# The last supertiles' units: second half rounded in two pieces, its subtraction and the fills put behind an addition

## The chip, the cores and the metric

The kernel runs on one core of a Trainium2 chip. TensorE (PE) multiplies matrices into PSUM; its weight loads have a row of their own in the profile (PEld). VectorE (DVE) and ScalarE (ACT) work element by element and read PSUM, GpSimd (POOL) does a little arithmetic and issues some DMAs, and SyncE (SP) issues the rest. Every engine executes its own instructions in order and waits for the others at semaphores. The metric is the time of one execution in microseconds; lower is better.

## The reference

An attention without softmax is followed by two feed-forward networks, each over all 2 x 3008 = 6016 tokens of width 256, with 2048 hidden columns:

```python
scores = scale * np.matmul(z, z.transpose(0, 2, 1))
attn = np.maximum(scores, 0.0) ** 2
out = np.matmul(attn, v)
x = u * out
...
h = x @ w_in1
g = h - np.tanh(h)
x = g @ w_out1
...
h = x @ w_in2
g = np.where(h >= 1, h, np.where(h <= -1, 0.0, (h + 1) ** 2 / 4))
return g @ w_out2
```

The weights come as 64-bit floats and are turned into 32-bit ones on the chip.

## The kernel before

After the attention (440 us of the span) the two networks run one after the other. The tokens are cut into six **supertiles** of 1024, the last of 896, and each supertile into two halves of columns: 512, and in the last supertile 448 (`w`). The 2048 hidden columns are cut into eight blocks of 256 (`f`). A **unit** is one block of one supertile of one network. Units are numbered through: the first network has units 0 to 47, its last supertile 40 to 47; the second has 48 to 94, its last supertile 88 to 94 (the very last block has code of its own, `end_s` and `end_av`).

A value is held as two parts, hi (rounded) and lo (the rest, by a subtraction), and a product takes three matmuls (`mult`). The four products of a 2 x 2 block multiplication are saved down to seven, by sums of blocks: Y holds A11, then has S2, S3 and A22 added to it one after another, X holds A12, and V holds S1 and later S4. Since Y goes on being added to, ScalarE takes a **snapshot** of it before each addition: m1 after A11, u2 after S2, u3 after S3 (`snap`; tiles `m` and `u` in the trace), and the half B takes a copy after A22 (`hb<-m`). VectorE adds: `ha<-m` is X + m1, `ha<-u` is V + u3, `hb<-u` is V + u2. TensorE may write S2 into Y only when m1 is taken, S3 only after u2, A22 only after u3, and S4 into V only after `ha<-u`.

The unit's two halves A and B (tiles `ha`, `hb`) then pass through the network's function in `Half`: `first` (tanh on ScalarE in the first network, a clamp on VectorE in the second), `square` (second network, ScalarE), `value` (VectorE, `ta` or `tb`), `round` (ScalarE, hi: `gha`, `ghb`), `rest` (VectorE, lo: `gla`, `glb`). Their products with `w_out` (`parts`) are multiplied in the next unit, between the next unit's own blocks: eight matmuls with gha after S2, four with gla and six with ghb after S3, two more with ghb and four with glb after S4. The six with ghb take its second 512 or 448 columns first (four matmuls), then the first (two).

The order is written out by hand in `emit`, with `self` the unit and `p` the one before it, whose half B is finished here. In the first network ScalarE rounds half A at the end of its own unit (`if not self.late`), ahead of the next unit's m1; in the second network it does so in the next unit, behind m1. Work that belongs to no unit is called by `fill`, twice in a unit: steps that prepare the next supertile's inputs (tiles `xh`, `xl`, `t`), the conversion of the second network's weights (`win`, `wout`, `ein`, `eout`, `min`, `mout`, `phin`, `plin`, `phout`, `plout`), and the transposes of finished output tiles (`ot<-y`). One unit in each supertile of the second network but its first, unit 89 in the last one, has `before` set and an order of its own, since two banks of the finished supertile are emptied in it.

Of the kernel before, what the change touches and what calls it, by code (L numbers as in the profile page):

```python
# [8 lines left out]
F32R = mybir.dt.float32r  # L9
# [6 lines left out]
P = 128  # L16
# [6 lines left out]
QT = 512  # L23
# [8 lines left out]
def attention_then_two_ffn(  # L32
# [40 lines left out]
    sp_p = ctx.enter_context(tc.tile_pool(name="split", bufs=3))  # L73
# [31 lines left out]
    def flush():  # L105
        for fn in deferred:
            fn()
        deferred.clear()
# [614 lines left out]
    def fill():  # L723

        if fills:
            step = fills.pop(0)
            for fn in step:
                if fn is not None:
                    fn()
            if len(step) == 1:  # L730
                work(CONVERT[1] / 2)
        else:
            work(CONVERT[1])
        due()

    def copy(out_, in_):
        nc.scalar.activation(out=out_, in_=in_, func=AF.Copy)  # L737

    def add(out_, x, bank):
        nc.vector.tensor_tensor(out=out_, in0=x, in1=bank, op=ALU.add)  # L740

    class Half:
# [26 lines left out]
                out=t, in0=self.h[self.at(j)], in1=t, op=ALU.subtract if self.net == 0 else ALU.max,  # L769
            )  # L770

        def round(self, js=(None,)):
            self.hi = sp_p.tile([P, 2, 512], F32R, tag="hi", name=f"gh{self.nm}")
            for j in js:
                copy(self.hi[self.at(j)], self.t[self.at(j)])

# [15 lines left out]
    class Unit:  # L792
# [59 lines left out]
        def emit(self, p, att=None):  # L852

            w = self.w
            before = p and p.net == 1 and p.f == 0 and p.s and p.before
            self.before = p
            self.late = self.net == 1 or att is not None
            one, two, three = p.parts_list if p else ([], [], [])
            Y = self.bank()
            self.mult(Y, A11, "b11", True)  # L860
            m1 = self.snap("m1", Y)
            if p and p.late:
                p.A.round()
            if p and p.before and p.before.net == 0:
                p.before.empty(0)
            X = self.bank()
            self.mult(X, A12, "b21", True)
            if p:
                if p.net == 1:
                    p.B.first()  # L870
                p.A.rest()
                p.B.first() if p.net == 0 else p.B.square(1 if before else None)
            if att:
                for fn in att[2][:5]:
                    fn()
            self.A = Half(self.net, w, "a")
            if not (p and p.late):
                add(self.A.h[:, 0, :w], m1, X[:, :w])
            V = self.bank()
            self.mult(V, S1, "t1", True)  # L880
            if att:
                for fn in att[2][5:]:
                    fn()
                got = []
                inside.append(lambda: self.mult(Y, S2, "t2"))
                inside.append(lambda: got.append(self.snap("u2", Y)))
                att[0]()
                u2 = got[0]
            else:
                self.mult(Y, S2, "t2")  # L890
                u2 = self.snap("u2", Y)
            if before:
                before.empty(1, lambda: p.B.square(0))
            if p:
                for j in (1, 0) if before else (None,):
                    p.B.value(j)
                if p.late:
                    add(self.A.h[:, 0, :w], m1, X[:, :w])
            for fn in one[:4] if before else one:
                fn()  # L900
            if p:
                p.B.round((1, 0) if before else (None,))
                if self.i > 1:
                    fill()
                else:
                    scales.pop()()
                    due()
                    due()
                p.B.rest()
            self.mult(Y, S3, "t3")  # L910
            if before:
                for fn in one[4:6] + two[:2] + one[6:]:
                    fn()
                two = two[2:]
            u3 = self.snap("u3", Y)
            add(self.A.h[:, 1, :w], u3, V[:, :w])
            if self.net == 1 or att:
                self.A.first()
            for fn in two:
                fn()  # L920
            if att:
                self.A.value()
                att[1]()
            if self.i > 1:
                fill()
            if self.net == 1:
                self.A.square()
            self.mult(Y, A22, "t4")
            self.mult(V, S4, "b22")
            self.B = Half(self.net, w, "b")  # L930
            if self.net == 0 and not att:
                self.A.first()
            copy(self.B.h[:, 1, :w], Y[:, :w])
            if not att:
                self.A.value()
            if att:
                flush()
            add(self.B.h[:, 0, :w], u2, V[:, :w])
            for fn in three:
                fn()  # L940
            if not self.late:
                self.A.round()
            if p and p.net == 1:
                p.empty(0)
            self.parts_list = self.parts()
# [178 lines left out]
    with tc.manual_schedule():  # L1124
# [64 lines left out]
        def work(amount):  # L1189

            if not (converts or posts):
                return
            state["credit"] = min(state["credit"] + amount, 2.0)
            if posts:
                cost, fn = posts.pop(0)
                fn()
                state["credit"] -= cost
            while converts and state["credit"] > 0 and len(posts) < 3:
                if state["step"] == 0:
                    next(converts[0])  # L1200
                elif state["step"] == 1 and len(converts) > 1:
                    next(converts[1])
                state["step"] += 1
                cost = next(converts[0], None)
                if cost is None:
                    converts.pop(0)
                    state["step"] = 1
                else:
                    state["credit"] -= cost
# [45 lines left out]
        def due():  # L1255

            now = [fn for k, fn in later if k <= 0]
            later[:] = [(k - 1, fn) for k, fn in later if k > 0]
            for fn in now:
                fn()  # L1260
# [73 lines left out]
        p = None  # L1334
        for i, (net, s, f) in enumerate(units):
            if f == 0:
                more = (net, s + 1) if (net, s + 1, 0) in units else (1, 0) if net == 0 else None
# [9 lines left out]
            p = u  # L1347
# [70 lines left out]
```

## Time and profile before

| | |
|---|---|
| time, median of 3 runs | 1420.18 us (1419.55 to 1420.5) |
| the profiled execution's own time | 1417.62 us |
| its span, first to last instruction | 1415.8 us |
| TensorE matmuls, weight loads busy | 99%, 83% |
| VectorE, ScalarE, GpSimd busy | 88%, 70%, 8% |
| granted TensorE clock, mean | 0.999 |

Matmuls are pipelined and their ends are modelled, so a matmul row of 0.37 us may stand beside the next one 0.20 us later. "Idle before" in a row is the time the engine stood still ahead of it, with what ended that time.

### The profile page before, as it was taken

How to read it: one execution, taken by the hardware profiler on the slowest of the kernel's cores; microseconds unless marked ns; L12 is line 12 of the kernel's file. 1: busy time of each engine (PE TensorE's matmuls, PEld its weight loads, DVE VectorE, ACT ScalarE, POOL GpSimd, SP SyncE). 2: the span in 40 equal slices, each digit the busy share in tenths (PEclk: the TensorE clock that was granted, in tenths of full speed). 3: DMA queues.
4: the chain of work that ended last, by engine and by line, in shares of the span. 5: the costliest groups of instructions: out<-in, count | busy, mean ns of one | idle time of the engine just before them, and what ended most of it. 6: DMA issues, size and time to landing. Idle time of an engine off the chain costs nothing.

```text
span 1415.8 us, 21846 instructions
## 1 busy us (share of the span) xinstructions
PE 1408.6 (99%) x8206; PEld 1173.7 (83%) x8206; DVE 1243.9 (88%) x1557; ACT 996.3 (70%) x1258; POOL 116.0 (8%) x169
## 2 busy tenths in 40 slices
PE   9999999999999999999999999999999999999998
PEld 7888888888888888888888889988888888888897
DVE  8888899788898989899889889989898898988887
ACT  8888758888765767667676767666666666666664
POOL 0111110022110010110201110000000000000000
PEclk9999999999999999999999999999999999999999
DMA  8788897599989557484847667572564653546461
GB/s 231 249 279 256 234 237 190 177 283 270 257 220 318 198 195 254 167 309 134 314 147 271 230 224 276 173 289 89 176 225 178 208 189 109 184 157 222 148 208 27
DMA packets 229546, 301.02 MB, mean 213 GB/s; under 512 B 111152, under 2 KB 166192, under 8 KB 229440
## 3 DMA queue, kind: packets, MB, share of 16 engines
q1 hardware_dynamic: 213088, 258.01, 57.6%
q0 software_dynamic: 11520, 40.96, 8.1%
q8 instruction: 64, 1.05, 0.3%
q10 hardware_dynamic: 4832, 0.66, 0.3%
q14 instruction: 42, 0.34, 0.1%
HBM read 225.77 MB, written 73.79 MB: 212 GB/s over the span
## 4 chain that ended last, share of the span: by engine, by line
PE 60%; issue 36%; DVE 1%; ACT 1%; DMA 1%; POOL 0%; SPq 0%; POOLq 0%; DVEq 0%; ACTq 0%
PE acc L825 17%; PE acc L537 16%; PE m L806 15%; PE acc L526 7%; PE sc L449 4%; DMA packed<-plin 0%; ACT r L475 0%; PE acc L532 0%; DVE lo L434 0%; PE warm L1122 0%; ACT hi L483 0%; DVE am L416 0%; POOL win L282 0%; POOL packed L295 0%; DVE lo L499 0%
## 5 line engine op out<-in xcount | busy, mean ns | idle before, releaser
L806 PE MATMUL m<-xht,w 128*128 128x512 f32 (+1 forms) x760 | 231.2, 385 | 0.0
L825 PE MATMUL acc<-ghb,w 128*128 128x512 f32 (+1 forms) x760 | 200.8, 386 | 0.0
L537 PE MATMUL acc<-hi,v 64*128 64x512 f32 (+1 forms) x1588 | 195.5, 382 | 0.2
L825 PE MATMUL acc<-gha,w 128*128 128x512 f32 (+1 forms) x760 | 187.1, 386 | 0.0
L537 PEld LDWEIGHTS acc<-hi,v 64*128 64x128 f32 x1588 | 148.5, 184 | 29.2 <-DVE y L592 1.3
L825 PEld LDWEIGHTS acc<-gha,w 128*128 128x128 f32 x760 | 142.4, 188 | 27.5 <-ACT y L737 0.4
L825 PEld LDWEIGHTS acc<-ghb,w 128*128 128x128 f32 x760 | 141.2, 188 | 29.0 <-ACT ghb L737 0.7
L806 PEld LDWEIGHTS m<-xht,w 128*128 128x128 f32 x760 | 142.7, 188 | 26.4
L806 PE MATMUL m<-xlt,w 128*128 128x512 f32 (+1 forms) x380 | 147.2, 387 | 0.0
L779 DVE TENSOR_TENSOR gla<-ta,gha 128x1024 fp32r<-128x1024 f32 (+1 forms) x95 | 114.4, 1204 | 36.7 <-ACT gha L737 36.0
L737 ACT ACTIVATE ghb<-tb 128x1024 fp32r<-128x1024 f32 (+3 forms) x100 | 99.8, 1004 | 63.0 <-DVE tb L768 63.0
L768 DVE TENSOR_TENSOR ta<-ha,ta 128x1024 f32<-128x1024 f32 (+1 forms) x95 | 114.2, 1202 | 32.6 <-ACT ta L764 27.5
L779 DVE TENSOR_TENSOR glb<-tb,ghb 128x1024 fp32r<-128x1024 f32 (+1 forms) x95 | 114.0, 1200 | 18.1 <-ACT ghb L737 17.9
L737 ACT ACTIVATE u<-m 128x512 f32<-128x512 f32 (+1 forms) x190 | 110.3, 580 | 26.3 <-PE m L806 25.4
L737 ACT ACTIVATE gha<-ta 128x1024 fp32r<-128x1024 f32 (+1 forms) x95 | 98.9, 1041 | 35.0 <-DVE ta L768 34.8
L768 DVE TENSOR_TENSOR tb<-hb,tb 128x1024 f32<-128x1024 f32 (+3 forms) x100 | 114.7, 1147 | 6.5 <-ACT tb L753 2.2
L806 PE MATMUL m<-xhb,w 128*128 128x512 f32 (+1 forms) x380 | 115.6, 386 | 0.0
L764 ACT ACTIVATE ta<-ta 128x1024 f32<-128x1024 f32 (+1 forms) x47 | 49.2, 1046 | 85.4 <-DVE ta L755 85.4
L537 PE MATMUL acc<-lo,v 64*128 64x512 f32 (+1 forms) x772 | 104.9, 382 | 0.2 <-DVE lo L434 0.2
L475 ACT ACTIVATE r<-sc 128x1024 f32<-128x1024 f32 (+1 forms) x83 | 84.4, 1016 | 28.4 <-PE sc L449 28.0
L825 PE MATMUL acc<-gla,w 128*128 128x512 f32 (+1 forms) x380 | 101.3, 386 | 0.0
L825 PE MATMUL acc<-glb,w 128*128 128x512 f32 (+1 forms) x380 | 101.1, 385 | 0.0
(139 smaller groups left out, 2566.1 us busy)
## 6 DMA issues: line engine op xcount, KB each, us to landing
w<-packed SPq DMA_DIRECT2D x288, 512.0 KB, 5.9
mir<-ax SPq DMA_DIRECT2D x50, 512.0 KB, 4.6
m<-mir SPq DMA_DIRECT2D x200, 128.0 KB, 4.6
xr<-kept SPq DMA_DIRECT2D x20, 512.0 KB, 6.9
packed<-phin POOLq DMA_DIRECT2D x16, 512.0 KB, 5.7
packed<-plin POOLq DMA_DIRECT2D x16, 512.0 KB, 6.1
widein<-in_moe_w_in_dram POOLq DMA_DIRECT2D x15, 512.0 KB, 6.9
wideout<-in_moe_w_out_dram POOLq DMA_DIRECT2D x15, 512.0 KB, 7.7
```

What stands on the lines that cost most here:

```text
L449: nc.tensor.matmul(ps[:, j, :n], zs[b, g][half, x, k0 : k0 + P], q[half, y, :n], start=(k == 0), stop=(k == 2))
L475: nc.scalar.activation(out=r[s], in_=ps[s], func=AF.Relu)
L526: nc.tensor.matmul(acc[d][h].rearrange("p (i q) -> p i q", i=2), lhsT, g[half, j], start=start, stop=stop)
L537: nc.tensor.matmul(acc[d][h][:, :n], lhsT, g[half, j, :n], start=start, stop=stop and (h == 1 or not closes))
L737: nc.scalar.activation(out=out_, in_=in_, func=AF.Copy)
L764: nc.scalar.activation(out=t, in_=t, func=AF.Square, scale=0.5, bias=0.5)
L768: nc.vector.tensor_tensor(out=t, in0=self.h[self.at(j)], in1=t, op=ALU.subtract if self.net == 0 else ALU.max,)
L779: nc.vector.tensor_tensor(out=self.lo[self.s], in0=self.t[self.s], in1=self.hi.bitcast(F32)[self.s], op=ALU.subtract)
L806: nc.tensor.matmul(bank[:, : self.w], self.win[wp][:, block, :], xop[self.net, self.s][x][xp], start=start and i == 0, stop=True, skip_gro ...
L825: nc.tensor.matmul(self.acc(d, n)[:, : self.w], self.wout[:, part, j, d * P : (d + 1) * P], g[:, at, : self.w], start=start, stop=stop,)
```

## The change

In the units of 448 columns except unit 89 (`narrow`), the one ScalarE instruction that rounds half B becomes two: the second columns' piece stands where the whole one stood, and the first columns' piece stands behind snapshot u3. The subtraction for glb and the first call of `fill` move behind the addition `ha<-u`. Unit 89 and the units of 512 columns keep the order of the rounding and of glb; unit 89 no longer has its first call of `fill`, since that branch now asks for 512 columns, so what stood there is taken by the next call.

```diff
--- before.py
+++ after.py
@@ -769,8 +769,9 @@
                 out=t, in0=self.h[self.at(j)], in1=t, op=ALU.subtract if self.net == 0 else ALU.max,
             )
 
-        def round(self, js=(None,)):
-            self.hi = sp_p.tile([P, 2, 512], F32R, tag="hi", name=f"gh{self.nm}")
+        def round(self, js=(None,), more=False):
+            if not more:
+                self.hi = sp_p.tile([P, 2, 512], F32R, tag="hi", name=f"gh{self.nm}")
             for j in js:
                 copy(self.hi[self.at(j)], self.t[self.at(j)])
 
@@ -856,6 +857,7 @@
             self.before = p
             self.late = self.net == 1 or att is not None
             one, two, three = p.parts_list if p else ([], [], [])
+            narrow = w < QT and not before
             Y = self.bank()
             self.mult(Y, A11, "b11", True)
             m1 = self.snap("m1", Y)
@@ -899,21 +901,27 @@
             for fn in one[:4] if before else one:
                 fn()
             if p:
-                p.B.round((1, 0) if before else (None,))
-                if self.i > 1:
-                    fill()
-                else:
+                p.B.round((1, 0) if before else (1,) if narrow else (None,))
+                if self.i <= 1:
                     scales.pop()()
                     due()
                     due()
-                p.B.rest()
+                elif w == QT:
+                    fill()
+                if not narrow:
+                    p.B.rest()
             self.mult(Y, S3, "t3")
             if before:
                 for fn in one[4:6] + two[:2] + one[6:]:
                     fn()
                 two = two[2:]
             u3 = self.snap("u3", Y)
+            if narrow:
+                p.B.round((0,), more=True)
             add(self.A.h[:, 1, :w], u3, V[:, :w])
+            if narrow:
+                p.B.rest()
+                fill()
             if self.net == 1 or att:
                 self.A.first()
             for fn in two:
```

TensorE's instructions keep their order. In VectorE's, this is unit 43 in the first network before, from the value of half B (`tb`) to the addition for its own half B (`hb`); L779 is the subtraction for glb, and `xlb`, `t` and `plout` are fills:

```order
L768 TENSOR_TENSOR tb<-hb,tb 128x2x448
L695 TENSOR_TENSOR xlb_0_10385<-xr_0_0_10046,xhb_0_10298 128x1024
L779 TENSOR_TENSOR glb<-tb,ghb 128x2x448
L740 TENSOR_TENSOR ha<-u_10394,m 128x448
L658 TENSOR_TENSOR t_0_10407<-xr_0_1_10047,t_0_10296 128x512
L291 TENSOR_TENSOR plout_6_10409<-wout_6_10226,phout_6_10319 128x512
L768 TENSOR_TENSOR ta<-ha,ta 128x2x448
L740 TENSOR_TENSOR hb<-u_10372,m 128x448
```

The same place after the change:

```order
L768 TENSOR_TENSOR tb<-hb,tb 128x2x448
L740 TENSOR_TENSOR ha<-u_10391,m 128x448
L780 TENSOR_TENSOR glb<-tb,ghb 128x2x448
L695 TENSOR_TENSOR xlb_0_10397<-xr_0_0_10046,xhb_0_10309 128x1024
L658 TENSOR_TENSOR t_0_10411<-xr_0_1_10047,t_0_10307 128x512
L291 TENSOR_TENSOR plout_6_10413<-wout_6_10228,phout_6_10322 128x512
L768 TENSOR_TENSOR ta<-ha,ta 128x2x448
L740 TENSOR_TENSOR hb<-u_10375,m 128x448
```

The addition `ha<-u` now stands right behind `tb`, and glb and the fill `xlb` stand between it and `ta`.

ScalarE's order in unit 43 before, from snapshot u2 to the next unit's m1 (`xht` is a fill):

```order
L737 ACTIVATE u_10372<-m 128x448
L737 ACTIVATE ghb<-tb 128x2x448
L679 ACTIVATE xht_0_10387<-t_0_10296 128x1024
L737 ACTIVATE u_10394<-m 128x448
L753 ACTIVATE ta<-ha 128x2x448
L737 ACTIVATE hb<-m 128x448
L737 ACTIVATE gha<-ta 128x2x448
L737 ACTIVATE m_10443<-m 128x448
```

And after the change:

```order
L737 ACTIVATE u_10375<-m 128x448
L737 ACTIVATE ghb<-tb 128x448
L737 ACTIVATE u_10391<-m 128x448
L737 ACTIVATE ghb<-tb 128x448
L679 ACTIVATE xht_0_10399<-t_0_10307 128x1024
L753 ACTIVATE ta<-ha 128x2x448
L737 ACTIVATE hb<-m 128x448
L737 ACTIVATE gha<-ta 128x2x448
L737 ACTIVATE m_10447<-m 128x448
```

The rounding of half B is cut around u3, the fill `xht` stands behind both, and gha still stands ahead of the next m1.

VectorE's order in the second network's units 89 and 90 before, from `ha<-m` of unit 89 to `ta` of unit 90 (`ot<-y` are the transposes of finished output):

```order
L740 TENSOR_TENSOR ha<-m_14459,m 128x448
L973 STREAM_TRANSPOSE ot<-y_14445 128x512
L779 TENSOR_TENSOR glb<-tb,ghb 128x2x448
L740 TENSOR_TENSOR ha<-u_14514,m 128x448
L755 TENSOR_SCALAR ta<-ha 128x2x448
L973 STREAM_TRANSPOSE ot<-y_14447 128x512
...
L740 TENSOR_TENSOR ha<-m_14563,m 128x448
L973 STREAM_TRANSPOSE ot<-y_14483 128x512
L779 TENSOR_TENSOR glb<-tb,ghb 128x2x448
L740 TENSOR_TENSOR ha<-u_14604,m 128x448
L755 TENSOR_SCALAR ta<-ha 128x2x448
L973 STREAM_TRANSPOSE ot<-y_14486 128x512
```

And after the change:

```order
L740 TENSOR_TENSOR ha<-m_14468,m 128x448
L780 TENSOR_TENSOR glb<-tb,ghb 128x2x448
L740 TENSOR_TENSOR ha<-u_14522,m 128x448
L755 TENSOR_SCALAR ta<-ha 128x2x448
L981 STREAM_TRANSPOSE ot<-y_14454 128x512
...
L740 TENSOR_TENSOR ha<-m_14563,m 128x448
L740 TENSOR_TENSOR ha<-u_14601,m 128x448
L780 TENSOR_TENSOR glb<-tb,ghb 128x2x448
L981 STREAM_TRANSPOSE ot<-y_14456 128x512
L755 TENSOR_SCALAR ta<-ha 128x2x448
L981 STREAM_TRANSPOSE ot<-y_14492 128x512
```

Unit 89 has one transpose fewer, the second one of unit 90 is what was its first, and the last goes to unit 91.

## Rows read from the trace of the kernel before

**Rows 1.** The page, busy time by engine, whole span.

```profile
PE 1408.6 (99%) x8206; PEld 1173.7 (83%) x8206; DVE 1243.9 (88%) x1557; ACT 996.3 (70%) x1258; POOL 116.0 (8%) x169
```

**Rows 2.** Busy time by stretch: unit 43, stretch, length, each engine's busy time.

```profile
core 0: us, PE busy (x) PEld busy (x) DVE busy (x) ACT busy (x) POOL busy (x), PEclk, DMA share, GB/s
875.27:884.39 9.12, 9.12 (x47) 8.45 (x46) 8.37 (x12) 6.62 (x10) 0.54 (x1) 1.00 0.47 188
```

**Rows 3.** Waits of TensorE's weight loads, 847.2 to 923.4: total, times, longest.

```profile
PEld m L806 <- ACT m L737: 0.2, 1, 0.2
```

**Rows 4.** Waits in the second network's last units, 1330.1 to 1395.3.

```profile
PEld m L806 <- DVE ha L740: 0.3, 1, 0.3
PEld acc L825 <- ACT ghb L737: 0.3, 1, 0.3
PEld m L806 <- ACT u L737: 0.2, 1, 0.2
```

**Rows 5.** In order of time, unit 43: start, length, engine, instruction.

```profile
875.39 0.95 ACT L737 ACTIVATE gha<-ta 128x896 fp32r<-128x896 f32 x1 [1.04 <-DVE ta L768]
876.25 0.52 ACT L737 ACTIVATE m<-m 128x448 f32<-128x448 f32 x1
876.89 0.19 PEld L806 LDWEIGHTS m<-xlt,w 128*128 128x128 f32 x1
...
878.92 1.22 DVE L695 TENSOR_TENSOR xlb<-xr,xhb 128x1024 fp32r<-128x1024 f32 x1
...
879.52 0.57 PE L806 MATMUL m<-xht,w 128*128 128x448 f32 x2
...
880.05 1.08 DVE L779 TENSOR_TENSOR glb<-tb,ghb 128x896 fp32r<-128x896 f32 x1
880.54 1.20 PEld L825 LDWEIGHTS acc<-ghb,w 128*128 128x128 f32 x6
...
881.40 0.62 DVE L740 TENSOR_TENSOR ha<-u,m 128x448 f32<-128x448 f32 x1 [0.26 <-ACT u L737]
881.94 0.69 DVE L658 TENSOR_TENSOR t<-xr,t 128x512 f32<-128x512 f32 x1
882.54 0.68 DVE L291 TENSOR_TENSOR plout<-wout,phout 128x512 fp32r<-128x512 f32 x1
883.14 1.08 DVE L768 TENSOR_TENSOR ta<-ha,ta 128x896 f32<-128x896 f32 x1
```

**Rows 6.** VectorE's groups, 847.2 to 920.9: first and last of 22 fills.

```profile
L695 DVE TENSOR_TENSOR xlt<-t,xht 128x1024 fp32r<-128x1024 f32 x2 | 2.4, 1218 | 0.0
...
L250 DVE TENSOR_SCALAR ein<-widein 128x512 uint32<-128x512 uint32 x1 | 0.4, 418 | 0.0
```

**Rows 7.** In order of time, unit 15.

```profile
592.39 1.06 ACT L737 ACTIVATE gha<-ta 128x1024 fp32r<-128x1024 f32 x1 [1.80 <-DVE ta L768]
...
593.36 0.58 ACT L737 ACTIVATE m<-m 128x512 f32<-128x512 f32 x1
...
593.99 0.19 PEld L806 LDWEIGHTS m<-xlt,w 128*128 128x128 f32 x1 [0.43 <-ACT m L737]
...
594.33 0.62 PE L806 MATMUL m<-xht,w 128*128 128x512 f32 x2
```

**Rows 8.** In order of time, units 40 and 41.

```profile
850.74 0.42 DVE L250 TENSOR_SCALAR eout<-wideout 128x512 uint32<-128x512 uint32 x1
...
851.73 0.57 PE L806 MATMUL m<-xht,w 128*128 128x448 f32 x2
...
852.34 0.54 ACT L737 ACTIVATE u<-m 128x448 f32<-128x448 f32 x1 [0.41 <-PE m L806]
...
858.65 0.19 PEld L806 LDWEIGHTS m<-xlt,w 128*128 128x128 f32 x1
```

**Rows 9.** In order of time, unit 89.

```profile
1344.60 0.59 ACT L737 ACTIVATE ghb<-tb 128x448 fp32r<-128x448 f32 x1
1345.35 0.70 DVE L973 STREAM_TRANSPOSE ot<-y 128x512 f32<-128x512 f32 x1
...
1347.61 0.30 PEld L806 LDWEIGHTS m<-xhc,w 128*128 128x128 f32 x2 [0.27 <-DVE ha L740]
```

## The prediction

> **What bounds the kernel now.** I read the page's first part, then the stretches of the last supertiles by unit, then the waits in them, then single instructions in order of time. The page has TensorE's matmuls busy 99% of the span [rows 1]. A narrow unit of the first network (448 columns, units 40 to 47) has 21 + 24 = 45 matmuls and lasts 9.12 us, 0.203 us each, with VectorE busy 8.4 us of it and ScalarE 6.6 (the row of unit 43; 41 to 46 are alike to 0.01 us in length) [rows 2]. The waits say whether TensorE loses anything there: in all eight narrow units of the first network its weight loads wait 0.2 us in total [rows 3], in the second network's last units 0.3 + 0.3 + 0.2 us [rows 4]. So all that the two last supertiles could give back is about 1.0 us, 0.07% of the time. What matters is therefore not what the change takes away but whether it makes TensorE wait where it doesn't now.
>
> For that one follows the ring of dependences that joins one unit to the next. In rows of unit 43 and what stands round it [rows 5]: snapshot m1 (876.25) lets TensorE write bank Y again (S2, weight load at 876.89, 0.12 us after m1's end at 876.77); then eight gha matmuls and S3, ended at 880.09; snapshot u3; VectorE's addition h1 (`ha<-u`); the subtraction `ta` that makes the half's value; its rounding gha on ScalarE; and behind gha, in ScalarE's order, the next unit's m1. In the first network gha stands ahead of m1. A late `ta` thus delays m1, and m1 delays S2. Unit 15 shows that it bites: gha waited 1.80 us for `ta`, m1 came at 593.36, and S2's weight load stood 0.43 us waiting for m1 [rows 7].
>
> **The change part by part.**
>
> *The split rounding.* One ScalarE instruction of 0.95 us [rows 5] becomes two of 0.59 [rows 9]; consecutive ones overlap by 0.09 (gha is 0.95 long, m1 starts 0.86 after it), so 0.1 us more ScalarE work in each of 14 units, on an engine with 2.5 us to spare in a unit [rows 2]. The snapshot u3 no longer stands behind the whole rounding and a filling rounding (xht before), only behind a half. The second half must be there for the fifth ghb matmul. u3 starts 0.04 us after S3's end, as at 852.34 [rows 8]; S3's end is 880.09, so the second piece ends at about 880.09 + 0.04 + 0.45 + 0.59 = 881.17, while the fifth of the ghb loads would come at 880.54 + 4 x 0.20 = 881.34. With 0.05 us for the signal, 0.12 us remain. Cost nothing; cover gone, it would cost what it is late, once a unit.
>
> *The subtraction glb and the fills behind the addition.* This is the part that counts. VectorE runs in order. Before, between the second half's value `tb` and the addition h1 it did the first fill and glb (in unit 43, xlb from 878.92 and glb from 880.05) while TensorE was still at gha and S3; h1 then started at 881.40. After, h1 is next behind `tb` and waits for u3; behind it are queued glb, both fills, and then `ta`, for which ScalarE's gha and the next m1 wait. VectorE's wait for u3 is empty, and what used to fill it now stands on the ring.
>
> The ring after, for unit 43, each piece from its row [rows 5, 7]:
> - `ta`'s end to gha 0.04 (as S3's end to u, 851.73 + 0.57 to 852.34 [rows 8]), gha to m1's start 875.39 to 876.25: 0.90
> - m1 0.52, to S2's weight load 0.05 (593.36 + 0.58 to 593.99): 0.57
> - S2's load to S3's end 880.09 - 876.89 = 3.20, less 0.09, since after a wait the second matmul follows its block's load by 0.34 (593.99 to 594.33) where 0.20 + 0.23 would be the pace of 512 columns: 3.11
> - u3 0.04 + 0.54 [rows 8], h1 0.04 + 0.54 (881.40 to 881.94): 1.16
> - glb 1.08, of which the next one overlaps 0.08 (xlb is 1.22 long, and glb starts 1.13 after it): 1.00
> - the fills: xlb 1.13, t 0.60, plout 0.60: 2.33
> - `ta` 1.08
>
> Sum 10.15, against 9.12 for a unit: 1.03 us lost. Without its fills the ring is 7.82. In the order of before, glb and xlb are not in it: 10.15 - 1.00 - 1.13 = 8.02, 1.1 us to spare, which is why no wait shows there now. A unit loses nothing only while its fills take under 1.30 us.
>
> Over the eight units of that supertile the fills are 32 instructions in 22 groups, together 22.3 us busy, from 2.4 us for two down to 0.4 us for one [rows 6]; with 0.08 us of overlap each that is 19.7 us on the ring. The lightest unit, 45, has one fill like t and one like xlb, 0.60 + 1.13 = 1.73 us, and still loses. Eight turns: 8 x 7.82 + 19.7 - 8 x 9.12 = 9.3 us. The first turn starts from undisturbed times [rows 8]: u3 at 852.34, h1 at 852.92, glb from 853.46 (1.00 x 512/448 = 1.14 for the wide half), four fills like the one at 850.74 (0.34 each) and two like t (0.60) to 857.16, `ta` ended 858.24, m1 859.14, S2's load 859.71 where it stood at 858.65: 1.06 - 0.09 = 0.97, where the formula has 2.56 + 7.82 - 9.12 = 1.26. That takes off 0.3: **9.0 us**. Seven of the eight waits fall in units 41 to 47, the eighth at S2 of unit 48. Bounds: 0.2 us a turn either way for the small pieces and for fills that are slower beside GpSimd's sums, so 7.4 to 10.6; below that only if the ring doesn't close (rivals).
>
> *Units 88 and 90 to 94.* In the second network gha stands behind m1, and hardly any fills are left (an xhd in 88, four transposes). So glb ahead of `ta` or behind it is the same sum, and h1 comes no later than its slack allows. The small waits on ghb in 88 (0.3 in [rows 4]) should go: some 0.1 us of TensorE's time.
>
> *Unit 89*, whose order is the special one, loses its first fill: the transpose of 0.70 us at 1345.35 moves to the next place, so that glb and h1 come some 0.3 us earlier and the wait of 0.27 us for h1 at 1347.61 [rows 9] goes; in time about 0.16. The two transposes pushed into 90 and one into 91 put 0.7 us ahead of `ta` there; m1 doesn't wait for it, gha has about half a microsecond: 0 to 0.5 lost. Output stores go out one fill later on SP's queue, behind the next weights and not ahead of them; nothing waits for them. Taken together the second network gives -0.2, between -0.6 and +0.6.
>
> *Sum.* +9.0 - 0.2 = +8.8 us. Profiled execution: span 1415.8, its own time 1417.6, so 1426.4 for such an execution; the median of the timed runs is 2.6 above it, so 1420.2 + 8.8 = **1429.0 us**, 0.6% slower.
>
> **Rivals.**
>
> *No change, 1420.0 (7%).* The ring doesn't close: somewhere in it there is slack that I don't see. For it: the chain had 1.1 us to spare, and the lateness must exceed that. Against: m1's end stands only 0.12 us before S2's load, and the fills of every unit are over 1.30 us. Then only the second network's -0.2 would remain.
>
> *Faster (3%).* The earlier h1 and u3 take away TensorE's waits: that can give at most the 1.0 us of [rows 3, 4], 1419.2, within 0.2% and hence no measurable gain. A larger gain needs TensorE to have room that its busy time hides. Weight loads are busy 8.45 of 9.12 us in these units [rows 2]; were that idle 0.67 us a loss by late operands, 14 units would hold 9.4 us, 1410.8. Against it: the loads come 0.20 us apart inside one block as well, where nothing is waited for (six of ghb in 1.20 us [rows 5]), and the rows of waits say 0.2 and 0.8 us. The Trainium skill (Perfetto Trace Analysis, Identifying the Most-Contended Engine) says that matmul busy time is a poor measure of headroom and that the busy share of the weight loads is a good one; by that rule these units would have the 8% that this rival gives back, and the trace doesn't agree that it can be won by earlier operands.
>
> *Slower for another reason.* The second rounding piece comes after the fifth ghb load: 14 times the lateness; it decides from 0.2 us each (2.8 us in all, 1423.0) and would show as waits on ghb. I count it in the range, under 5%.
>
> **How the numbers follow.** The likeliest is the ring: 1429.0, chance about 0.87, and 0.03 more for slower by the late piece. The range takes 7.4 to 10.6 with the second network's bounds, and half a microsecond for the spread of the runs: 1426.0 to 1431.2. About 0.2% of the time is what a measurement of this kernel can tell from no change: faster 0.03, same 0.07, slower 0.90.
>
> **What would show it.** Right: units 41 to 47 some 9.5 to 11 us long instead of 9.12; weight loads of S2 waiting for m1 eight times, some 0.4 to 2 us each; VectorE idle 1 to 2 us before `ha<-u` in each, waiting for u3; gha waiting for `ta`; units 90 to 94 at 9.13 as before; unit 89 a little shorter. Wrong: units 41 to 47 still 9.12 us; or waits on ghb or h1 in place of m1; or the fills no longer on VectorE between h1 and `ta`.

## The result

| | before | changed |
|---|---|---|
| time, median of 6 runs | 1420.09 us (1419.25 to 1420.61) | 1428.45 us (1427.68 to 1429.51) |
| the profiled execution's own time | 1417.62 us | 1428.3 us |
| its span | 1415.8 us | 1426.5 us |

The ratio is 1.006, with a 95% interval of 1.0047 to 1.0073: slower by 8.4 us, where 8.8 were predicted. The two profiled executions stand 10.7 us apart, more than the medians, since the one of before lies 2.5 us below its median and the one of after doesn't. Differences of single units below are from this pair.

The page's first part shows almost nothing of it, in the form of [rows 1]:

```profile
PE 1412.0 (99%) x8206; PEld 1173.7 (82%) x8206; DVE 1244.1 (87%) x1557; ACT 997.2 (70%) x1272; POOL 115.6 (8%) x169
```

TensorE is "99% busy" again; 14 more instructions on ScalarE are the roundings cut in two. The loss shows only by unit. Busy time by stretch, for units 41, 43, 44 and 47, as [rows 2] for unit 43 before:

```profile
core 0: us, PE busy (x) PEld busy (x) DVE busy (x) ACT busy (x) POOL busy (x), PEclk, DMA share, GB/s
857.02:867.39 10.37, 9.49 (x46) 8.25 (x46) 9.29 (x13) 6.60 (x11) 0.20 (x1) 1.00 0.54 171
877.76:887.57 9.81, 9.39 (x47) 8.37 (x46) 7.78 (x11) 6.59 (x10) 0.00 (x0) 1.00 0.40 153
887.57:897.72 10.15, 9.38 (x47) 8.38 (x46) 8.12 (x11) 6.26 (x10) 0.54 (x1) 1.00 0.40 129
917.43:928.98 11.55, 9.38 (x47) 8.37 (x46) 9.48 (x13) 6.59 (x10) 2.49 (x5) 1.00 1.01 351
```

Each of these units lasted 9.12 us before. Matmuls and weight loads have the same work in all; the granted clock is 1.00; no engine is full. So something waits. The waits from 847.2 to 931 (total us, times, longest), where [rows 3] had one of 0.2 us for m1:

```profile
ACT gha L737 <- DVE ta L768: 17.1, 8, 3.7
...
DVE ha L740 <- ACT u L737: 12.4, 8, 2.1
...
PEld m L807 <- ACT m L737: 8.8, 7, 2.5
```

VectorE stands idle 12.4 us in front of `ha<-u`, waiting for u3; ScalarE then waits 17.1 us for `ta` in front of gha; TensorE's S2 waits for m1. Seven such waits are in the list; the eighth, in unit 48, lies behind this stretch. In order of time, one turn, from gha ahead of unit 43's m1 to the weight load behind the next m1 (before: [rows 5]):

```profile
879.02 0.95 ACT L737 ACTIVATE gha<-ta 128x896 fp32r<-128x896 f32 x1 [1.48 <-DVE ta L768]
...
879.88 0.52 ACT L737 ACTIVATE m<-m 128x448 f32<-128x448 f32 x1
...
880.45 0.19 PEld L807 LDWEIGHTS m<-xlt,w 128*128 128x128 f32 x1 [0.80 <-ACT m L737]
...
883.59 0.55 ACT L737 ACTIVATE u<-m 128x448 f32<-128x448 f32 x1 [0.35 <-PE m L807]
884.00 1.20 PEld L826 LDWEIGHTS acc<-ghb,w 128*128 128x128 f32 x6
884.03 0.57 ACT L737 ACTIVATE ghb<-tb 128x448 fp32r<-128x448 f32 x1
884.17 0.62 DVE L740 TENSOR_TENSOR ha<-u,m 128x448 f32<-128x448 f32 x1 [1.54 <-ACT u L737]
...
884.71 1.08 DVE L780 TENSOR_TENSOR glb<-tb,ghb 128x896 fp32r<-128x896 f32 x1
...
885.71 1.22 DVE L695 TENSOR_TENSOR xlb<-xr,xhb 128x1024 fp32r<-128x1024 f32 x1
...
886.85 0.69 DVE L658 TENSOR_TENSOR t<-xr,t 128x512 f32<-128x512 f32 x1
...
887.45 0.69 DVE L291 TENSOR_TENSOR plout<-wout,phout 128x512 fp32r<-128x512 f32 x1
...
888.05 1.09 DVE L768 TENSOR_TENSOR ta<-ha,ta 128x896 f32<-128x896 f32 x1
...
889.17 0.95 ACT L737 ACTIVATE gha<-ta 128x896 fp32r<-128x896 f32 x1 [2.33 <-DVE ta L768]
...
890.02 0.52 ACT L737 ACTIVATE m<-m 128x448 f32<-128x448 f32 x1
...
890.60 0.19 PEld L807 LDWEIGHTS m<-xlt,w 128*128 128x128 f32 x1 [1.14 <-ACT m L737]
```

Read the idle times in brackets from the top: VectorE waits 1.54 us for u3 with glb and the fills queued behind the waiting addition; then it does them one after the other without a gap, 884.71 to 888.05; `ta` follows; ScalarE has waited 2.33 us for it; m1 stands behind gha. From one m1 to the next it is 890.02 - 879.88 = 10.14 us; the prediction's ring had 10.15 for this unit.

What one unit's turn loses shows in the next unit, whose S2 has to wait. Unit by unit the change costs +1.24, +1.25, +0.69, +1.03, +1.03, +0.43, +2.44 and +1.37 us in units 41 to 48, together 9.48. Units 50 to 87, which it doesn't touch, differ by 0.6 in this pair; units 88 to 93 by +0.1 in sum. So the units give 9.6 us where the medians give 8.4; what makes up the rest wasn't followed.

### The profile page after: what moved, and what is told of

It is laid out like the page before. It is cut to its first block, busy times and chain, and to the rows that moved or that the text cites. A ratio compares the mean times of both kernels' runs of the same rounds, so it can differ in the third digit from the quotient of the medians.

```text
span 1426.5 us, 21870 instructions
## 1 busy us (share of the span) xinstructions
PE 1412.0 (99%) x8206; PEld 1173.7 (82%) x8206; DVE 1244.1 (87%) x1557; ACT 997.2 (70%) x1272; POOL 115.6 (8%) x169
## 4 chain that ended last, share of the span: by engine, by line
PE 59%; issue 36%; DVE 3%; ACT 1%; POOL 0%; DMA 0%; POOLq 0%; SPq 0%; DVEq 0%
PE acc L537 17%; PE acc L826 16%; PE m L807 14%; PE acc L526 7%; PE sc L449 4%; DVE glb L780 1%; DVE ta L768 0%; PE acc L532 0%; PE warm L1130 0%; ACT u L737 0%; DVE lo L434 0%; DMA m<-mir 0%; DVE am L416 0%; ACT gha L737 0%; ACT m L737 0%
## 5 line engine op out<-in xcount | busy, mean ns | idle before, releaser
L737 ACT ACTIVATE ghb<-tb 128x1024 fp32r<-128x1024 f32 (+2 forms) x114 | 102.6, 905 | 64.7 <-DVE tb L768 64.7
```

## The experiments

Theory A is the prediction's: what counts is the loops of in-order waits that join one unit to the next, and how much of the moved work stands on one of them. Its rivals are told in the expectations. The first four kernels were run together, beside 23 runs of the kernel before (median 1420.49 us), the last three beside 13 (1419.87). Diffs are against the kernel before or the changed one, as said.

**1. The change in the second network alone** (against the changed kernel).

```diff
-            narrow = w < QT and not before
+            narrow = self.net == 1 and w < QT and not before
...
-                elif w == QT:
+                elif w == QT or self.net == 0:
                     fill()
```

> The change in the second network's last supertile alone (units 88 to 94); the first network's units keep the order of before. Theory A, the ring of the first network (ta, gha, next m1, S2, S3, u3, ha<-u, glb, fills, ta): all of the loss goes, time within 0.2% of before, 1419.5 to 1420.5, units 41 to 47 at 9.12 us. Theory B, the moves cost in every narrow unit alike (one more ScalarE instruction, a late second half): about 6 of 14 parts of the loss stay, +3 to +4 us, 1423 to 1424.

Measured: 1420.11 us, ratio 0.9999 (0.999 to 1.0007); units 41 to 48 as before to 0.07 us in sum. The whole loss is the first network's last supertile, and in the second network the same edits are worth nothing. Their small effect on waits is seen there; TensorE's waits in that kernel's last units, beside [rows 4]:

```profile
PEld m L807 <- ACT u L737: 0.6, 3, 0.2
PEld acc L826 <- ACT gha L737: 0.3, 1, 0.3
```

The waits for ghb and for `ha<-u` are gone, and waits for u2 and gha of the same size stand in their place.

**2. The first fill put back** (against the changed kernel): split rounding and glb stay behind u3 and `ha<-u`.

```diff
-                elif w == QT:
+                elif w == QT or narrow:
                     fill()
...
             if narrow:
                 p.B.rest()
-                fill()
```

> The change with the first call of fill put back ahead of ha<-u; the split rounding and glb behind ha<-u stay. Theory A: the turn keeps only the second fill, 7.82 + 1.2 to 2.2 us, and loses nothing where that is under 9.12; units with more lose some 0.1 to 0.9 us, and a ScalarE fill ahead of u3 adds up to 0.4: +1 to +2.5 us, 1421 to 1422.6. Theory B (split rounding or glb's place): it stays at 1427 to 1429.

Measured: 1422.0 us, ratio 1.0007 (0.9998 to 1.0017). By unit, 41 to 48 cost +2.61 us in its profile, the most (1.06) at unit 47, behind the long second call of unit 46. TensorE's waits from 847 to 926:

```profile
PEld m L807 <- ACT m L737: 1.7, 3, 1.0
PEld acc L826 <- ACT ghb L737: 0.8, 3, 0.3
```

So one call of `fill` less between `ha<-u` and `ta` takes 6.9 of the 8.4 us away, with the split rounding and the late glb both still there. The 1.5 us that are left are not all the second call's. In unit 43 the ring with that call alone would be 7.82 + 1.20 = 9.02 and lose nothing; yet `ta` comes 9.49 us after the last one, and unit 44 lost 0.29. With the call ScalarE's fill xht is back ahead of u3:

```profile
881.31 0.58 ACT L737 ACTIVATE ghb<-tb 128x448 fp32r<-128x448 f32 x1 [0.76 <-DVE tb L768]
881.80 1.04 ACT L679 ACTIVATE xht<-t 128x1024 fp32r<-128x1024 f32 x1
882.75 0.52 ACT L737 ACTIVATE u<-m 128x448 f32<-128x448 f32 x1
```

The three waits for ghb are all at the fifth load, 0.23 to 0.34 us each: there the second piece of the split rounding, behind that late u3, came too late.

**3. Only the first fill moved** (against the kernel before).

```diff
                 if self.i > 1:
-                    fill()
+                    if w == QT:
+                        fill()
...
             add(self.A.h[:, 1, :w], u3, V[:, :w])
+            if w < QT and not before:
+                fill()
```

> Before, with only the first call of fill moved behind ha<-u in the narrow units; the rounding is whole and glb stays ahead of ha<-u. Theory A: glb (1.0 us) is done while u3 is waited for, but delays ha<-u by about 0.3; a turn is 7.1 us and its fills of 1.7 to 3.4, so units lose 0 to 1.5 us: +2 to +5 us, 1422 to 1425, more than nothing and less than the change. Theory B: no loss, 1420.

Measured: 1425.74 us, ratio 1.0035 (1.0021 to 1.0049), 0.7 above the upper end. Where the rest comes from is in the waits of its narrow units:

```profile
DVE glb L779 <- ACT ghb L737: 8.3, 8, 1.1
PEld m L806 <- ACT m L737: 5.9, 7, 1.9
```

With the fill gone from in front of it, glb waits for the rounding ghb, 8 times about 1 us, and `ha<-u` stands behind it. That is a second loop, which I had not counted: end of `ta`, gha 0.04 + 0.95, gla 0.04 + 1.00, `ha<-m` 0.54, `tb` 1.08, ghb 0.04 + 0.95, glb 0.04 + 1.00, `ha<-u` 0.54, fills, `ta` 1.08: 7.30 us and the fills. With the 2.33 of unit 43 it makes 9.63, a loss of 0.51 a unit; units 44 and 45 lost 0.51 each. One turn of VectorE and ScalarE in that kernel:

```profile
877.88 1.09 DVE L768 TENSOR_TENSOR ta<-ha,ta 128x896 f32<-128x896 f32 x1
...
881.52 1.08 DVE L768 TENSOR_TENSOR tb<-hb,tb 128x896 f32<-128x896 f32 x1
882.64 0.95 ACT L737 ACTIVATE ghb<-tb 128x896 fp32r<-128x896 f32 x1 [0.75 <-DVE tb L768]
...
883.63 1.09 DVE L779 TENSOR_TENSOR glb<-tb,ghb 128x896 fp32r<-128x896 f32 x1 [1.02 <-ACT ghb L737]
...
887.51 1.08 DVE L768 TENSOR_TENSOR ta<-ha,ta 128x896 f32<-128x896 f32 x1
```

`ta` starts at 877.88 and again at 887.51: 9.63 us.

**4. The ring opened at gha** (against the changed kernel): in the narrow units of the first network gha is rounded behind the next m1, as the second network does.

```diff
+            self.lag = self.net == 0 and w < QT
...
-            if p and p.late:
+            if p and (p.late or p.lag):
                 p.A.round()
...
-            if not self.late:
+            if not (self.late or self.lag):
                 self.A.round()
```

> The change, with gha of the first network's narrow units rounded in the next unit behind m1, as the second network has it. VectorE's order is that of the change. Theory A: the link ta to gha to m1 to S2 is cut; what is left is ta to gha to the eight gha matmuls, 1.04 us shorter, so a turn loses that much less: +1 to +3.5 us, 1421 to 1423.6, waits of S2 for m1 gone, a few waits for gha in their place. Theory C, VectorE simply has too much work in these units or waits too long for u3: the loss stays, 1427 to 1429.

Measured: 1425.08 us, ratio 1.0033 (1.0021 to 1.0045). Theory A expected more back (1423.6 at most), Theory C nothing. TensorE's waits, 847 to 932:

```profile
PEld acc L826 <- ACT gha L737: 3.6, 5, 1.8
PEld acc L826 <- ACT ghb L737: 3.5, 14, 0.4
```

S2 doesn't wait for m1 any more, as the ring has it, but 3.8 us came back (8.4 less 4.6) and not more, since a third loop stands right behind: `ha<-u` 0.54, glb 1.00, fills, `ta` 1.08, gha with its signals 1.03, gla 1.00, `ha<-m` 0.54, `tb` 1.08, first piece of ghb 0.54, u3 0.54, signal 0.04: 7.39 us and the fills. In this kernel u3 stands behind a piece of ghb, which waits for `tb`. With 2.33 us of fills it makes 9.72, 0.60 lost; measured 0.57 and 0.56 in units 44 and 45. Seven of the 14 waits for ghb are at its first load (0.24 to 0.35 us), for the piece behind the late `tb`. The other seven, at the fifth load (0.18 to 0.20 us), are the lateness of the second piece that the prediction named; they show once the wait for m1 no longer comes first.

**5 and 6. A dose** (against the kernel before): the subtraction for glb done once more, and twice more, behind `ha<-u`, in the eight units. The work repeats one with the same result and writes the same values.

```diff
             add(self.A.h[:, 1, :w], u3, V[:, :w])
+            if self.net == 0 and w < QT:
+                for _ in range(1):
+                    p.B.again()
```

> The kernel before, in which the eight units of the first network's last supertile do the subtraction glb a second time, with the same values, right behind the addition ha<-u; everything else stays where it was. Theory A (loops of in-order waits, with known slack): two loops that before have slack take the extra 1.00 us. The loop through m1 was 6.82 plus the second fill, about 8.0 us, so it goes to 9.0 and still fits into 9.12. The loop through ghb, glb and ha<-u was 7.30 us plus the second fill plus what the first fill takes beyond 0.99, in unit 43 8.64 us; it goes to 9.64 and loses 0.5 us a unit. Over the eight units about +4.5, so 1423 to 1426, and the waits are of glb for ghb or of h1, few of S2 for m1. Theory B (VectorE has room for the work, it matters only how busy it is): net of overlaps VectorE does 7.4 us in a unit of 9.12, so 1.0 more fits: 1420. Theory C (each microsecond behind ha<-u costs one at once): eight times 1.0, 1428.

> As the kernel with one repetition, with the subtraction repeated twice. Theory A: no slack is left in either loop, so the second repetition costs its whole 1.00 us in each of eight turns: 8 us above the kernel with one, 1431 to 1434.5, and units of 10 to 11 us. Theory B: VectorE's work net of overlaps would be 9.4 of 9.12 us, 0.3 too much in each of eight units: 1422.5. Theory C: 16 us above before, 1436.

Measured: 1426.23 us, ratio 1.0042 (1.0025 to 1.0059), with one; 1434.74 us, 1.0103 (1.0088 to 1.0118), with two. Theory B, VectorE's load, is out: it had no loss at all for one. Theory C, a full microsecond from the first, is 1.8 too high for one and 1.3 for two, though inside both intervals (up to 8.4 and 16.8 us); the units 41 to 48 of the two profiles speak against it with +6.57 and +15.11 us. Theory A comes nearest, at 0.2 above its range both times. Its point is that the first microsecond is partly covered by slack and the second isn't: the medians give 6.4 us for the first and 8.5 for the second, where eight units of 1.00 would be 8. What it left out for the first is again a branch of a loop; unit 43 with one repetition:

```profile
882.67 1.04 ACT L679 ACTIVATE xht<-t 128x1024 fp32r<-128x1024 f32 x1
...
883.62 0.53 ACT L737 ACTIVATE u<-m 128x448 f32<-128x448 f32 x1
884.18 0.62 DVE L740 TENSOR_TENSOR ha<-u,m 128x448 f32<-128x448 f32 x1 [0.26 <-ACT u L737]
```

ScalarE does its own fill between ghb and u3, and so `ha<-u` waits for u3 another 0.26 us, in four units 1.0 us. That is about half of the difference between 4.5 and 6.4; the rest wasn't followed. The waits were not those that were expected either: glb waited for ghb in two of these units only, 0.8 us in all, and TensorE's S2 for m1 in seven, 7.1 us.

With two repetitions TensorE waits at another place too, since the repeated subtraction writes the tile that it reads (847.2 to 935):

```profile
PEld m L811 <- ACT m L737: 8.1, 7, 1.6
PEld acc L830 <- DVE glb L784: 6.3, 7, 1.1
```

In each turn the wait for glb comes first and S2 still waits 1.0 to 1.6 us for m1 behind it, so the loop, not this wait, sets the time.

**7. The same work at another place** (against the changed kernel): the moved call of `fill` stands behind the last addition of half B, that is behind `ta`.

```diff
             if narrow:
                 p.B.rest()
-                fill()
+                if self.net == 1:
+                    fill()
...
             add(self.B.h[:, 0, :w], u2, V[:, :w])
+            if narrow and self.net == 0:
+                fill()
```

> The change, but in the first network's narrow units the first fill is called behind the last addition of half B, that is behind ta, where VectorE waits for the rounding gha anyway, and not between ha<-u and ta. VectorE does exactly the same work, and glb stays behind ha<-u. Theory A: the loop through m1 is 7.82 us plus the second fill alone, which is 1.13 to 1.27 us in most units and so fits into 9.12 or nearly; the loop through gha, gla and the second half's value is 7.39 us plus the second fill plus what the first takes beyond about 0.5: small losses in units 40 to 45, together some 0.6 us, and about 2 in units 46 and 47, whose fills are longer. So +1 to +3.5, 1421 to 1423.5. Theory B (it costs whatever place behind ha<-u the fills stand at, or the split rounding itself costs): as the change, 1427 to 1429.

Measured: 1421.49 us, ratio 1.0011 (1.0002 to 1.002). The turn of unit 43 again:

```profile
882.42 0.62 DVE L740 TENSOR_TENSOR ha<-u,m 128x448 f32<-128x448 f32 x1 [1.09 <-ACT u L737]
...
883.96 1.22 DVE L695 TENSOR_TENSOR xlb<-xr,xhb 128x1024 fp32r<-128x1024 f32 x1
...
885.10 1.09 DVE L768 TENSOR_TENSOR ta<-ha,ta 128x896 f32<-128x896 f32 x1
...
886.63 0.69 DVE L658 TENSOR_TENSOR t<-xr,t 128x512 f32<-128x512 f32 x1
...
887.23 0.69 DVE L291 TENSOR_TENSOR plout<-wout,phout 128x512 fp32r<-128x512 f32 x1
887.84 1.09 DVE L780 TENSOR_TENSOR gla<-ta,gha 128x896 fp32r<-128x896 f32 x1
```

VectorE does the same instructions as in the changed kernel. The fills `t` and `plout` now lie between `ta` and gla, where it had stood idle 0.49 us for gha anyway, and units 43 to 46 are 9.12 us long again, to 0.01. Units 41, 47 and 48, behind the units with the longest fills, still lose (0.97, 0.94, 0.34), and unit 42 loses 0.09. TensorE's waits there are for ghb, 2.8 us from 847 to 935, and only 0.2 for m1. Some four fifths of the change's loss (8.4 us against 1.6) are the place of one call of `fill`. That is no price of the call alone: moved by itself it cost 5.2 us (experiment 3), the late glb and the split rounding without it 1.5 (experiment 2), and all together 8.4, since each uses up slack that the others would have had. No run has the split rounding by itself.

No kernel came out measurably below the kernel before, and none could by much: its waits there are the 1.0 us of [rows 3, 4].

## Why the prediction was right

*The ring.* The predicted 9.0 us are 9.48 in the profile. The pieces of the ring give the turns of units 43, 44 and 45 a loss of 1.03, 1.03 and 0.43 us (7.82 and 2.33, 2.33 and 1.73 of fills, less 9.12); the trace has 1.03, 1.03 and 0.43. Four of the eight were off:

- The first was 0.97 by the sum and 1.24 in the trace. Its fills took 2.75 us (854.87 to 857.62) and not 2.56, and the 0.09 for a block that starts late did not come off: in unit 41 S3 waited for u2, which ScalarE took behind two copies of a finished output tile (`y<-acc`).
- The same late S3 made the turn of unit 41 longer, 1.25 lost where its fills of 2.41 give 1.11.
- The turn of unit 46 lost 2.44 where its rows before (3.50 of fills) give 2.20; a slower `ta` took 0.27 more (last section), the fills 0.03 less.
- The turn of unit 47 was 10.81 long, as the ring has it (7.82 + 2.94), but lost 1.37 and not 1.64: the way from S2 of 47 to S2 of 48 had been 9.45 before and not 9.12, since unit 48 is 512 columns wide.

By the medians the loss is 8.4; the interval of the ratio, 6.7 to 10.4 us, holds both. That the median came within 0.4 of the forecast is in part chance, then: the units alone stand 0.8 above it. Three slips change nothing: unit 40 lasts 9.75 us before and not 9.12, the 0.2 us of [rows 3] are at S2 of unit 48, behind the narrow units, and 0.67 of 9.12 us is 7%, not 8%.

*The pieces of the change.* The prediction put glb and the fills together and gave them 1.00 + 2.33 us in unit 43. Experiments 2 and 7 show that the fills are what makes it longer than a unit: with one call less there most of the loss goes. In 7, in which one call is left there, in unit 43 xlb with 1.13 us, units 43 to 46 lose nothing, as the limit of 1.30 us of fills has it. From above, unit 45 of the changed kernel stands nearest to it: 1.73 us of fills, 0.43 lost.

*The split rounding at nothing.* Right in the changed kernel: the six ghb loads stand in one row of 1.20 us from 884.00, though the second piece starts at 884.03 only. Its cover is thin, as was said: the fifth load waited 0.2 us for it in seven units of experiment 4 and 0.2 to 0.3 in three of experiment 2.

*What the prediction didn't see.* The ring through m1 is not alone. Without their fills two others are 7.30 and 7.39 us long where it is 7.82: the one through ghb and glb (as the kernel of 3 has it) and the one through gla, `tb` and u3. For the forecast this was harmless, since the longest loop sets the time and it had been found. The expectations of 3 and 4, in whose kernels the longest was shortened or cut, missed because of them.

*The second network.* Predicted -0.2, between -0.6 and +0.6; in the trace +0.1, and -0.1 by the ratio of experiment 1 (-1.4 to +1.0). The waits on ghb in unit 88 and on `ha<-u` in 89 went, by 0.16 and 0.11 us; units 90 to 92, which should have stayed as before or lost little, gave 0.4 back, 92 by a wait of 0.2 for gha behind the transpose that was pushed on.

*The rival "faster".* Weight loads idle 0.67 us in a unit are no room to be won: experiment 1 moves `ha<-u` and u3 earlier in six of the second network's units and wins nothing (at most 1.4 us by its interval, where 0.67 in each would be 4). The Trainium skill (Perfetto Trace Analysis, Identifying the Most-Contended Engine) would read headroom from that idle share. The trace disagrees for these units: loads and matmuls both keep the matmuls' pace of 0.20 us inside a block.

## What to carry to other kernels

Where engines work in order, filling work belongs in front of an operation that waits, not behind it: there it is hidden by the wait, as long as it is over before the awaited event (ScalarE's fill in experiment 2 was not), and behind it stands between the awaited event and everything that hangs on the result. Before moving it, write down the loop from one unit to the next (and the second longest), add the moved work, and compare with the unit's length; busy shares say nothing here: the same VectorE work gave a unit of 10.15 us at one place and of 9.12 at another. Slack in a loop covers part of the first microsecond (6.4 us for eight) and hides what the second one will cost (8.5).

## What the runs showed of the hardware

GpSimd's sums and VectorE's instructions hold each other up, and in these rows the one that begins second pays. In unit 46 of the changed kernel GpSimd does four sums from 917.13 to 919.44, the last from 918.92:

```profile
916.89 0.42 DVE L250 TENSOR_SCALAR eout<-wideout 128x512 uint32<-128x512 uint32 x1
917.13 2.31 POOL L282 TENSOR_TENSOR win<-win 128x128 f32<-128x128 f32 x4 [28.16 <-DVE win L270]
917.23 0.69 DVE L252 TENSOR_SCALAR mout<-wideout 128x512 uint32<-128x512 uint32 x1
...
918.92 0.52 POOL L282 TENSOR_TENSOR win<-win 128x128 f32<-128x128 f32 x1
919.04 1.35 DVE L768 TENSOR_TENSOR ta<-ha,ta 128x896 f32<-128x896 f32 x1
```

The fill with one input that begins ahead of the sums takes 0.42 us, the next, of the same size, 0.69; `ta`, 1.09 in unit 43, begins behind the last sum and takes 1.35. In the kernel before, the subtraction glb begins ahead of the first sum:

```profile
907.19 1.08 DVE L779 TENSOR_TENSOR glb<-tb,ghb 128x896 fp32r<-128x896 f32 x1
907.42 1.17 POOL L282 TENSOR_TENSOR win<-win 128x128 f32<-128x128 f32 x1 [23.36 <-DVE win L270]
...
909.23 0.68 DVE L252 TENSOR_SCALAR mout<-wideout 128x512 uint32<-128x512 uint32 x1
```

It keeps its 1.08 us, and here it is the sum that takes longer, 1.17 us where the shortest of the four takes 0.46. The fills behind it are as slow as in the changed kernel. There it cost nothing, since the loop had slack. In the changed kernel they stand on the loop, and unit 47 is the longest of all, with 2.44 us lost: 7.82 + 3.47 for the fills from 915.57 to 919.04 + 0.27 for `ta` = 11.56, as measured. The Trainium skill (SBUF — State Buffer, Summary: rules for kernel authors) has the second of the two to issue wait until the first is done, where VectorE is in a mode that uses both its ports, or reads two inputs from SBUF while GpSimd reads there too. `ta` and glb agree in which of the two pays, though `ta` lost 0.27 us where 0.40 of the sum was left; whether the one-input fills use both ports no row shows.
